# Reordering the first ten microseconds of an attention + MLP block: modulation products ahead of the transposes, weights loaded in smaller pieces over two queues, and dummy matmuls gated by statistics

## Chip, cores and metric

The kernel runs on one core of one Trainium2 chip. The metric is device time of one execution in microseconds (us). Each profile gives the *span* too, from the first to the last recorded instruction; here the time is some 1.75 us longer than the span. Three executions of the kernel before took 560.24, 560.35 and 560.86 us.

## The reference

One transformer block with adaptive layer norm: 2048 tokens of width 512, 32 query heads on 8 key/value heads of width 128, and an MLP of 1792. Everything is bf16.

```python
mod = (silu(c) @ w_mod).reshape(1, 6, 1, -1)          # c: (1, 512), w_mod: (512, 3072)
sa, ca, ga, sb, cb, gb = (mod[:, i] for i in range(6))
h = layernorm(x) * (1 + ca) + sa                      # modulated norm
x = x + ga * attention(h, k_cache, v_cache, wq, wo)   # q = h @ wq, softmax(q k^T) v @ wo
h = layernorm(x) * (1 + cb) + sb
return x + gb * (relu(h @ w1) @ w2)
```

`attention` here reads the last 512 of the 2048 cached positions. The attention loop cannot start before the first query tile is there. That needs x (normalized), c (through silu and two of the six modulation products), and the first query weights.

## The kernel before

All that the change touches lies in the prologue. In the traces the engines run their instructions in the order in which the program adds them (the tensor engine of before: seven dummies from 1.04 us, c at 4.95, nine dummies from 5.06, transposes from 8.82, products from 9.04); a helper attaches the semaphore waits.

```python
def load_wm01(i, eng=None):                # two halves of the first two modulation matrices
    c0, c1 = i * DC // 2, (i + 1) * DC // 2
    dma(wm01[:, c0:c1, :], wm01v[:, c0:c1, :], f"wm{i}", writes=[R_wm[i]], eng=eng)

def warm(n):                               # dummies: nothing reads their result
    for i in range(n):
        mm(bank[WBK], ones[:, :], ones[:, 0:1].to_broadcast([P, QB]), True, True, [R_ones], [WBK], i == n - 1)
# ... cut: layer norm helpers, the attention loop, the MLP
for i in range(2):                         # x of the first 512 tokens, one half on each queue
    dma(x_sb[:, 2 * i:2 * i + 2, :], xv[:, 2 * i:2 * i + 2, :], f"xa{i}", writes=R_x[2 * i:2 * i + 2], eng=ACT if i else SP)
dma(c_row[:, :], c[0].rearrange("(c p) -> c p", p=P), "c", writes=[R_c])
load_wm01(0)
load_wm01(1, ACT)
load_wq(0, 2, ACT)                         # query weights of heads 0 and 1
load_wq(2, 2)
load_k(0)
load_v(0)
kb.op(POOL, lambda e: e.memset(ones[:, :], 1.0), writes=[R_ones])
# ... cut: identity and constants on GpSimd
warm(7)
silu_exp(5)                                # transpose of c on the tensor engine, exp(-c) and a copy on ScalarE
warm(9)
# ... cut: the statistics of token tile 3 on ScalarE
silu_mul()                                 # three operations on GpSimd: silu of c
ln_stat(0)                                 # statistics of tiles 0..2 on VectorE
ln_stat(1)
rstd_add(0, 2)
rstd_pow(0, 2)                             # power -1/2 on GpSimd
ln_stat(2)
rstd_add(2, 3)
rstd_pow(2, 4)
ln_norm(0)
ln_norm(1)                                 # VectorE; tile 3 is normalized by GpSimd
ln_tposes(0, TB[0])                        # four 128x128 transposes of tile 0
fs = mod_cols_mm(0, QBK)                   # 32 modulation products, one column each
for f in fs:
    f()
ln_norm(2)
mod_cols_evac(0, QBK)
for tl in range(1, TPB):
    ln_tposes(tl, TB[tl // 2])
mod_half(0, 0, DVE)                        # scale and shift on the way out of PSUM
mod_half(0, 2, ACT)
mod_half(0, 1, DVE)
mod_half(0, 3, ACT)
q_half(0, 0, CC_ORDER, QBK)                # first query halves
# ... cut: the other halves, then the loop
```

The dummies are there so that the tensor engine's clock is at full instead of half rate when the real work begins; in before's trace 512-wide matmuls start 0.43 us apart from 1.45 to 8.45 us and 0.21 to 0.22 us apart from 13.56 us on. That dummies bring the full rate is an assumption of mine.

## Time and profile before

| | before |
|---|---|
| time, three executions | 560.24, 560.35, 560.86 us |
| the profiled execution | 561.1 us, span 559.4 us |
| tensor engine busy | 98% of the span |
| first exponential of the loop (ScalarE) | 13.76 us after the start |

The lines are in the prediction below. A row of the timeline reads: start, busy time, engine, source line, operation, output <- inputs, shapes, how many were merged, and in brackets how long the engine had been idle and what ended it.

### The profile page before, as it was taken

To read this page: it belongs to the slowest core of one execution; us is meant where nothing else is said; L and a number is where in the kernel's file an instruction comes from. 1 tells how busy PE (TensorE), PEld (TensorE's weight loads), DVE (VectorE), ACT (ScalarE), POOL (GpSimd) and SP (SyncE) were. 2 spreads that over 40 slices of the span, in tenths; PEclk is the share of its full clock that TensorE was granted. 3 is DMA by queue.
4 is the path that set the end of the run, shared out by engine and by line. 5 is a ranking of instruction groups with operands and counts; after the bars stand their busy time and mean duration, and the time that the engine had idled before them with its cause. 6 is when DMAs were issued, how large, how long until landed. Compare 5 with 4: busy or idle time off the path is not lost.

```text
span 559.4 us, 9666 instructions
## 1 busy us (share of the span) xinstructions
PE 550.5 (98%) x4060; PEld 315.8 (56%) x4134; DVE 253.8 (45%) x551; ACT 348.9 (62%) x453; POOL 54.7 (10%) x53
## 2 busy tenths in 40 slices
PE   8999999999999999999999999999999999999998
PEld 4665555555555555555555555555555654444444
DVE  4455555553546544335445443333354448321134
ACT  4986666666666666666666666666666644432500
POOL 3000022004410000033000000332000000000000
DMA  9897763513114144352352412111215110210001
GB/s 268 248 207 174 143 169 46 114 39 76 40 38 76 39 73 117 58 133 57 94 95 57 76 40 39 39 39 38 39 39 76 39 30 0 44 34 23 22 29 47
DMA packets 113309, 42.67 MB, mean 76 GB/s; under 512 B 93928, under 2 KB 112104, under 8 KB 113256
## 3 DMA queue, kind: packets, MB, share of 16 engines
q1 hardware_dynamic: 112024, 40.82, 34.3%
q10 hardware_dynamic: 1232, 1.15, 0.6%
q8 instruction: 33, 0.54, 0.4%
q14 instruction: 20, 0.16, 0.1%
HBM read 18.35 MB, written 2.10 MB: 37 GB/s over the span
## 4 chain that ended last, share of the span: by engine, by line
PE 98%; issue 1%; DMA 1%; DVE 0%; SPq 0%; DVEq 0%
PE psS L1372 28%; PE psO L1372 27%; PE psQ L1372 23%; PE psW L1372 20%; DMA c_row<-in_c_dram 1%; DVE qT L1611 0%; DVE hT L1630 0%; SPq L1303 0%; DVE PT L1723 0%; DVE PT L1725 0%; PE psS L1375 0%; PE psO L1416 0%; DVE modc L1438 0%; DVEq L123 0%
## 5 line engine op out<-in xcount | busy, mean ns | idle before, releaser
L1493 ACT ACTIVATE PT<-psS 128x1024 bf16<-128x1024 f32 x256 | 262.7, 1028 | 128.2 <-PE psS L1372 128.1
L1372 PE MATMUL psS<-qT,kT 128*128 128x512 bf16 x508 | 150.9, 379 | 0.5 <-DVE qT L1611 0.4
L1372 PEld LDWEIGHTS psO<-v,PT 128*128 128x128 bf16 x2048 | 126.6, 98 | 30.2
L1372 PE MATMUL psO<-v,PT 128*128 128x129 bf16 x2048 | 137.0, 220 | 0.0
L1372 PE MATMUL psQ<-hT,wq 128*128 128x512 bf16 (+1 forms) x510 | 130.5, 377 | 0.3 <-DVE hT L1630 0.2
L1503 DVE RECIPROCAL rinv<-psO 128x4 f32<-128x4 f32 x128 | 23.3, 182 | 227.2 <-PE psO L1372 227.2
L1372 PE MATMUL psW<-wo,oT 128*128 128x512 bf16 x454 | 118.1, 379 | 3.0
L1504 DVE TENSOR_TENSOR o<-psO,rinv 128x512 bf16<-128x512 f32 x128 | 88.5, 691 | 4.9 <-DVE rinv L1503 0.5
L1372 PEld LDWEIGHTS psQ<-hT,wq 128*128 128x128 bf16 x512 | 49.9, 98 | 60.3 <-issue 0.6
L1372 PEld LDWEIGHTS psS<-qT,kT 128*128 128x128 bf16 x512 | 49.5, 98 | 58.9 <-ACT PT L1493 0.7
L1485 ACT ACTIVATE qT<-psQ 128x512 bf16<-128x512 f32 x126 | 74.7, 593 | 0.0
L1712 ACT ACTIVATE wq<-psS 128x512 bf16<-128x512 f32 x56 | 33.4, 597 | 49.3 <-PE psS L1372 48.9
L1372 PEld LDWEIGHTS psW<-wo,oT 128*128 128x128 bf16 x512 | 45.0, 98 | 32.9 <-DVE acc L1526 1.2
L1526 DVE TENSOR_TENSOR acc<-psW,acc 128x512 f32<-128x512 f32 x48 | 33.2, 691 | 6.5 <-PE psW L1372 6.5
L1372 PE MATMUL psO<-wmw,wq 128*128 128x512 bf16 (+1 forms) x165 | 32.8, 352 | 0.3
L1529 POOL TENSOR_TENSOR acc<-acc,gaf 128x512 f32<-128x512 f32 x12 | 15.6, 1303 | 146.7 <-DVE acc L1526 139.8
L1388 POOL TENSOR_TENSOR rstd<-rstd,cst 128x4 f32<-128x4 f32 x7 | 7.2, 1025 | 216.8 <-DVE rstd L1387 216.8
L1723 DVE TENSOR_TENSOR PT<-psO,gbf 128x512 f32<-128x512 f32 (+1 forms) x12 | 7.5, 624 | 40.4 <-PE psO L1372 40.4
L1372 PE MATMUL psS<-h2T,wmw 128*128 128x512 bf16 x109 | 25.0, 379 | 0.2
L1372 PEld LDWEIGHTS psO<-wmw,wq 128*128 128x128 bf16 x168 | 15.3, 98 | 16.5
L1372 PE MATMUL psS<-hT,wmw 128*128 128x512 bf16 x110 | 24.4, 379 | 0.1
L1382 DVE BATCH_NORM_STATS2 st<-x 128x6 f32<-128x512 bf16 x31 | 21.1, 681 | 4.8 <-DMA x<-in_A_x_dram 4.8
(85 smaller groups left out, 192.6 us busy)
## 6 DMA issues: line engine op xcount, KB each, us to landing
wo<-in_A_wo_dram SPq DMA_DIRECT2D x4, 1024.0 KB, 5.9
wq<-in_A_wq_dram SPq DMA_DIRECT2D x7, 512.0 KB, 4.6
wmw<-in_B_w_dram SPq DMA_DIRECT2D x14, 256.0 KB, 3.1
wmw<-in_w_mod_dram SPq DMA_DIRECT2D x5, 512.0 KB, 4.8
oT<-o SPq DMA_TRANSPOSE x128, 2.4
out_dram<-PT SPq DMA_DIRECT2D x15, 128.0 KB, 1.7
x<-in_A_x_dram SPq DMA_DIRECT2D x3, 512.0 KB, 4.3
v<-in_A_v_cache_dram SPq DMA_DIRECT2D x8, 128.0 KB, 3.8
```

What stands on the lines that cost most here:

```text
L1372: kb.op(PE, lambda e: e.matmul(out_ap, lhsT, rhs, start=start, stop=stop), reads=reads, group_writes=[R_b[k] for k in bk], signal=signal)
L1382: kb.op(DVE, lambda e: e.bn_stats(st[:, t, :], x_sb[:, t, :]), reads=[R_x[t]], writes=[R_st[t]])
L1388: kb.op(POOL, lambda e: e.tensor_tensor(rstd[:, sl], rstd[:, sl], cst[:, 0:1].to_broadcast([P, hi - lo]), op=ALU.pow), reads=R_rstd[sl] + ...
L1485: kb.op(ACT, lambda e: e.activation(qT[u % NQT][:, :], bank[bk], ACTF.Copy), reads=[R_b[bk]], writes=[R_qT[u % NQT]])
L1493: kb.op(ACT, lambda e: e.activation(PT[u % NPT][:, pr * 2:pr * 2 + 2, :], s_ps[pr][:, :, :], ACTF.Exp, scale=scale), reads=[R_b[pr * 2], R ...
L1503: kb.op(DVE, lambda e: e.reciprocal(rinv[:, u, :], o_ps[:, :, P]), reads=[R_b[5], R_b[6]], writes=[R_rinv])
L1504: kb.op(DVE, lambda e: e.tensor_tensor(o_sb[u % NOS][:, :, :], o_ps[:, :, 0:P], rinv[:, u, :].unsqueeze(2).to_broadcast([P, TPB, P]), op=A ...
L1526: kb.op(DVE, lambda e: e.tensor_tensor(acc[:, tl, :], bank[WBK], acc[:, tl, :], op=ALU.add), reads=[R_b[WBK], R_acc[tl]], writes=[R_acc[tl]])
L1529: kb.op(eng, lambda e: e.tensor_tensor(acc[:, tl, :], acc[:, tl, :], gaf[:, :], op=ALU.mult), reads=[R_acc[tl], R_ga], writes=[R_acc[tl]])
L1712: kb.op(ACT, lambda e: e.activation(h1T[b % 2][:, fc, :], bank[bk], ACTF.Relu), reads=[R_b[bk]], writes=[R_h1[b % 2][fc]], pre=all_events( ...
L1723: kb.op(DVE, lambda e: e.tensor_tensor(yt[i][:, c0:c1], bank[bk][:, c0:c1], gbf[:, c0:c1], op=ALU.mult), reads=[R_b[bk], R_gb], writes=[R_ ...
```

## The change

Its intent is to shorten the start: put the products where the tensor engine waits for normalization anyway, get the weights for them earlier, and have the tensor engine at full clock (512-wide matmuls 0.21 us apart, not 0.43) by means of dummies that do not stand in the way. The loads, in four and two pieces on alternating queues, and the ones set by VectorE:

```diff
-    load_wm01(0)
-    load_wm01(1, ACT)
-    load_wq(0, 2, ACT)
+    for i in range(DC):
+        load_wm01(i, (ACT, SP)[i % 2])
+    for i, eng in enumerate((ACT, SP)):
+        dma(wq_sb[:, 2 * i:2 * i + 2, 0:QA * Dh], wqv[:, 2 * i:2 * i + 2, 0:QA * Dh], f"wqa{i}", writes=[R_wqa[i]], eng=eng)
     load_wq(2, 2)
...
-    kb.op(POOL, lambda e: e.memset(ones[:, :], 1.0), writes=[R_ones])
+    kb.op(DVE, lambda e: e.memset(ones[:, :], 1.0), writes=[R_ones])
```

The dummies, and the order (cut: the helpers take a gate, and waits name the pieces instead of the halves):

```diff
-    warm(7)
+    warm(10)
     silu_exp(5)
-    warm(9)
...
     ln_stat(0)
+    warm(3, [R_mv[0]])
     ln_stat(1)
+    warm(2, [R_mv[1]])
...
-    ln_tposes(0, TB[0])
     fs = mod_cols_mm(0, QBK)
     for f in fs:
         f()
+    ln_tposes(0, TB[0])
+    mod_cols_evac(0, QBK)
     ln_norm(2)
-    mod_cols_evac(0, QBK)
...
-    for tl in range(1, TPB):
-        ln_tposes(tl, TB[tl // 2])
+    ln_tposes(1, TB[0])
+    warm(2, bk=6)
+    ln_tposes(2, TB[1])
+    ln_tposes(3, TB[1])
+    warm(1, bk=6)
```

Below, "the loads", "the order", "the gated dummies" (10, then 3 and 2) and "the dummies between" (2 and 1 among the transposes) name these parts.

More of the change, by code (lines that the diff above doesn't have):

```diff
@@ L1319, in build_fast @@
     R_q1 = RL("q1_", 2)
+    R_wmc = RL("wmc", DC)
+    R_wqa = RL("wqa", 2)
     R_cf, R_m01 = Res("cf"), Res("m01")
@@ L1350, in load_wm01 @@
     def load_wm01(i, eng=None):
-        c0, c1 = i * DC // 2, (i + 1) * DC // 2
-        dma(wm01[:, c0:c1, :], wm01v[:, c0:c1, :], f"wm{i}", writes=[R_wm[i]], eng=eng)
+        dma(wm01[:, i, :], wm01v[:, i, :], f"wmc{i}", writes=[R_wmc[i]], eng=eng)
     def wm_res(sl, cc):
-        return R_wm[cc // (DC // 2)] if sl < 2 else R_wm[sl]
+        return R_wmc[cc] if sl < 2 else R_wm[sl]
     def load_wo(j):
@@ L1363, in load_mlp @@
         if not wm_done:
-            wm_done.extend(all_events(R_wm))
+            wm_done.extend(all_events(R_wm + R_wmc))
         f0 = i % (FC // 2) * 2
@@ L1375, in tpose, with warm @@
         kb.op(PE, lambda e: e.transpose(out_ap, in_ap, ident[:, :]), reads=list(reads) + [R_ident], group_writes=[R_b[k] for k in bk], signal=signal)
-    def warm(n):
+    def warm(n, gate=(), bk=7):
         for i in range(n):
-            mm(bank[WBK], ones[:, :], ones[:, 0:1].to_broadcast([P, QB]), True, True, [R_ones], [WBK], i == n - 1)
+            mm(bank[bk], ones[:, :], ones[:, 0:1].to_broadcast([P, QB]), True, True, [R_ones] + list(gate), [bk], i == n - 1)
     def ln_stat(t):
@@ L1480, in q_mms @@
             mm(bank[bk], wq_sb[:, cc, h * Dh:(h + 1) * Dh], hT[b % 2][:, cc, :], i == 0, i == DC - 1,
-               [R_wq[h], R_hT[b % 2][cc]] + ([R_h0[cc]] if b == 0 else []), [bk], i == DC - 1)
+               (R_wqa if h < QA else [R_wq[h]]) + [R_hT[b % 2][cc]] + ([R_h0[cc]] if b == 0 else []), [bk], i == DC - 1)
         q_evac(u, bk)
@@ L1636, in q_half @@
             mm(bank[bk][:, hf * HB:(hf + 1) * HB], wq_sb[:, cc, u * Dh:(u + 1) * Dh], hT[0][:, cc, hf * HB:(hf + 1) * HB], cc == CC_ORDER[0], cc == CC_ORDER[-1],
-               [R_wq[u], R_half[hf][cc]], [bk], cc == CC_ORDER[-1])
-    for tl in range(1, TPB):
-        ln_tposes(tl, TB[tl // 2])
+               [R_wqa[cc // 2], R_half[hf][cc]], [bk], cc == CC_ORDER[-1])
+    ln_tposes(1, TB[0])
[3 more added lines that the diff above has]
+    warm(1, bk=6)
     mod_half(0, 0, DVE)
@@ L1712, in h1_group @@
         kb.op(ACT, lambda e: e.activation(h1T[b % 2][:, fc, :], bank[bk], ACTF.Relu), reads=[R_b[bk]], writes=[R_h1[b % 2][fc]],
-              pre=all_events(R_wq) if b < 2 else ())
+              pre=all_events(R_wq + R_wqa) if b < 2 else ())
     def y_group(b, tl, c0=0, c1=D, deng=None):
```

## The prediction

> **What bounds the kernel now.** I read the page first, then the chain of waits in order of time for the first 20 us, then the timeline of the first 30 us, then busy time and DMA by stretches of one microsecond. The page:
>
> ```profile
> span 559.4 us, 9666 instructions
> PE 550.5 (98%) x4060; PEld 315.8 (56%) x4134; DVE 253.8 (45%) x551; ACT 348.9 (62%) x453; POOL 54.7 (10%) x53
> PE 98%; issue 1%; DMA 1%; DVE 0%; SPq 0%; DVEq 0%
> ```
>
> The tensor engine is busy all the time and is 98% of the chain, so no other engine's speed matters except where it holds up the tensor engine. The diff touches nothing after the first two query projections: the attention loop, the output projection and the MLP keep their instructions and their order, as a listing of both kernels' instruction order confirms. What can change is therefore the start. The chain for it (start us, us, what):
>
> ```profile
> 1.24 3.66 DMA c_row<-in_c_dram
> 4.95 0.18 PE psO L1416
> 5.13 3.86 PE psW L1372 x9
> 8.98 0.22 PE psS L1375 x4
> 9.21 0.79 PE psQ L1372 x32
> 10.02 0.18 DVE modc L1438
> 10.30 0.42 DVE hT L1630
> 10.86 0.78 PE psQ L1372 x4
> 11.64 0.89 PE psO L1372 x8
> 12.55 0.44 DVE qT L1611
> 13.34 0.38 PE psS L1372
> ```
>
> psW x9 are dummy matmuls on a tile of ones, psS x4 the transposes of token tile 0, psQ x32 the modulation products, psQ/psO after them the first query halves; psS at 13.34 is the first score matmul, where the real loop begins. From there 559.4 - 13.34 = 546 us follow that the change leaves alone. So all that can be won lies in 13.34 us, 2.4% of the span, and a good part of that waits for x and c to land near 4.9 us. The timeline shows what the dummies hide (start us, us, engine line op tiles):
>
> ```profile
> 5.43 0.28 POOL L1421 TENSOR_SCALAR tmp<-tmp 128x4 f32<-128x4 f32 x1 [3.17 <-ACT c_f L1418]
> 5.80 1.04 POOL L1422 TENSOR_TENSOR tmp<-tmp,cst 128x4 f32<-128x4 f32 x1
> 6.92 0.20 POOL L1423 TENSOR_TENSOR sc_bf<-c_f,tmp 128x4 bf16<-128x4 f32 x1
> 7.08 1.51 POOL L1591 TENSOR_TENSOR rstd<-rstd,cst 128x2 f32<-128x2 f32 x2
> 7.82 1.22 DVE L1393 TENSOR_SCALAR xn<-x,mv,rstd 128x512 bf16<-128x512 bf16 x3
> 8.70 0.90 POOL L1604 TENSOR_SCALAR xn<-x,s,rstd 128x512 bf16<-128x512 bf16 x1
> 10.28 1.47 ACT L1632 ACTIVATE hT<-psS,modc 128x256 bf16<-128x256 bf16 x3 [2.87 <-PE psS L1375]
> ```
>
> Behind the dummies a second chain runs through GpSimd: silu of c (three operations, done at 7.12), two rstd powers, then the normalization of tile 3. VectorE has tile 0 normalized at about 7.82 + 0.41 = 8.23, but the tensor engine is inside its nine dummies until about 8.8. ScalarE then idles 2.87 us: it has no modulation before the products and their evacuation, and the products sit behind the transposes of tile 0.
>
> [...] in the early dummies the weight loads start 0.42 to 0.43 us apart, in the loop four 512-wide psQ matmuls take 1.02 us with one tail of 0.38, so (1.02 - 0.38)/3 = 0.21 us apart. (The granted-clock column says 1.00 in both, so I judge by spacing.) The doubling comes near the ninth dummy of the second group, at some 8.7 us. [...] 385, 378 and 366 GB/s in the three microseconds from 4 to 7[...].
>
> **The change, part by part.**
> *Loads.* The first two modulation matrices come in four quarters, alternating over both queues, instead of two halves, and the first two heads' query weights come in two halves, one per queue. Before, the later half of the modulation weights was issued at 1.66 us and took the longest of that tile's times to landing, 6.3 us: 7.9 us. After, x (0.52 MB) and the four quarters (1.05 MB) are first in line; the stretches move 0.03 MB to 2 us, 0.58 MB from 2 to 4 us, then 0.385, 0.378 and 0.366 MB per us, so 1.57 MB are there at about 6.6 us. Estimated landing 6.7 us instead of 7.9. By itself it saves nothing, as the products ran at 9.04; it allows the new order.
> *Ones set by VectorE instead of GpSimd.* First dummy at about 1.0 instead of 1.04 us: nothing.
> *Ten dummies instead of seven before the transpose of c.* 1.0 + 0.40 + 9 x 0.427 = 5.24 us, where c lands at 4.90. The transpose of c thus moves from 4.95 to about 5.24: 0.3 us later, and the whole GpSimd chain with it, as no slack is in it (silu done 7.42, first rstd pair 8.08, second 8.9, tile 3 normalized 9.0 to 9.9; VectorE's tile 0 at 8.12 to 8.53, tile 1 to 8.86). This is the cost that I think the change carries.
> *Nine dummies become 3 gated by tile 0's statistics and 2 gated by tile 1's.* With the statistics at 5.70 and 6.49 and full clock, they end near 6.4 and 6.95; at half clock 3 x 0.427 and 2 x 0.427 run to 7.03 and 7.88. Either way they no longer reach 8.8.
> *Products before the transposes.* They start at 7.47 (silu + 0.05), last 0.8 us (32 at 25 ns) and end near 8.3, while VectorE still normalizes. Removed from the path between transposes of tile 0 and the others: the 0.8 us. Evacuation goes between tile 1 and tile 2 on VectorE, at about 8.8 to 8.95.
> *Transposes and three more dummies.* Tile 0 at 8.6, tile 1 at 8.93 to 9.15; two dummies (0.43 us at full clock) to 9.6; tile 2 (normalized 8.97 to 9.38) to 9.82; tile 3 must wait for GpSimd's 9.9, so 10.0 to 10.22; one dummy to 10.43. The first two dummies fall into time in which tile 3 is awaited anyway; the last costs 0.2 us, except that the modulation of the first half finishes about then: VectorE 9.40 to 10.13 (0.33 us apart), ScalarE 9.40 to 10.42 (0.46 apart).
> *Query halves.* 10.43 instead of 10.86: eight matmuls at 0.11 to 11.3; the second half's modulations start at 10.46, when tile 3 is in PSUM, and VectorE's third ends at about 11.5 (before: 11.99); unit 0's second half ends at 11.68, before at 12.35. **Sum: 0.67 us earlier**, so the first score matmul at about 12.65 to 12.7.
> From there ScalarE (2 x 1.03 + 0.59 = 2.65 us a unit) and the tensor engine (8 x 0.215 + 16 x 0.057 = 2.63 us a unit) run as before and everything is shifted. 560.35 - 0.7 = 559.6 us.
>
> **The rivals.**
> *A, no delay of c:* if the clock opens inside the ten dummies[...], or c lands late as well, the 0.3 us fall away, tile 3 is ready at 9.6, and the score starts near 12.35: 559.3 us.[...]
> *B, the clock opens late or falls back:* the new second group is only 5 dummies with gaps[...]. If the array is at half clock at 10.4 us, sixteen 256-wide matmuls cost 16 x 0.107 = 1.7 us more and the first loop matmuls some more: 561 to 562.[...]
> *C, a load takes the place of the wait:* the K load is issued some 0.8 us later behind the extra issues on SyncE. Its bytes are still behind the same bytes, it took 7.2 us at most from 2.62, so 9.8, and even 10.6 is before 12.65. Query weights landed by 9.3 (2.1 + 7.1) before and are needed at 10.4. I expect no wait, 0.0 us.
> *D, gated on tile 3:* GpSimd's normalization is the bound whatever the order, and only the end of it counts: then gain is 10.46 - 10.2 = 0.2 us, and the time is 560.1. Against it: 0.8 us of products no longer stand in line with it, and the modulation of the first half no longer waits for the third tile.
>
> **How range and chances follow.** Sum 0.7, A 1.0, D 0.2, B a loss of 1 to 1.5. The three times before lie within 0.6 us of each other, so I take 558.7 to 560.7 as the range for 8 in 10, with 559.6 as the time. A gain of 2% would be 11.2 us, most of the prologue, 4.9 us of which are the landing of inputs: 1%. A loss of 2% needs the clock to stay at half for over 20 us: 1%. Within 2%: 98%.
>
> **What would show it.** Right: the transpose of c near 5.24 us; products from about 7.5 us and ahead of all transposes; no dummy running at 8.5 us; tile 3 the last awaited transpose, near 10.0; query halves from 10.4; first score matmul at 12.5 to 12.8; spacing 0.21 us in the loop from there and a span near 558.7. Wrong: dummies or query matmuls 0.43 (or 0.21 for 256 columns) apart after 9 us (B); products waiting for a quarter of the modulation weights after 7.5, or query matmuls for a DMA (C); c transposed at 4.95 (A); or a loop that takes more or less than 546 us, which my account excludes.

Its sum came to 0.67 us earlier, rounded to 0.7, and so to 560.35 - 0.7 = 559.6 us. Cut, as marked, are reasons that no run of this case shows: for what opens the clock and lets it fall back, and for how two queues share the transfers.

## The result

The changed kernel took 561.44 us in the median of six executions (560.75 to 562.79), the kernel before 560.54 us in its six (560.24 to 561.53). The ratio was 1.0016, with a 95% interval of 1.0002 to 1.0031. A ratio is the mean time of one kernel's runs over that of the other's of the same rounds, so it is not quite the ratio of these medians. The class predicted as all but certain, within 2%, came true; the direction did not. I had predicted 559.6 us and a range up to 560.7, and the result lies 1.8 us above the one and 0.7 above the other.

The page of the changed kernel has the same tensor engine, 98% busy:

```profile
span 559.6 us, 9674 instructions
PE 550.6 (98%) x4061; PEld 315.8 (56%) x4136; DVE 254.2 (45%) x552; ACT 349.1 (62%) x453; POOL 54.5 (10%) x52
PE 97%; DMA 1%; issue 1%; SPq 0%; DVE 0%
```

The chain of waits of the changed kernel at its start (start us, us, what):

```profile
2.06 6.91 DMA wmw<-in_w_mod_dram
...
9.01 0.35 PE psQ L1373 x8
9.36 0.47 PE psS L1376 x8
...
12.97 0.59 PE psS L1373 x2
```

Where the chain before went through nine dummies, it now goes through a load: the last quarter of the modulation weights, issued at 2.06 us, landed at 8.96 us, and the last eight products waited for it. The timeline of the changed kernel adds what came before:

```profile
1.11 4.45 PE L1373 MATMUL psW<-ones 128*128 128x512 bf16 x10 [1.11 <-DVE ones L1570]
5.49 0.18 PE L1417 MATMUL psO<-ident,c_row 4*128 4x4 bf16 x1
5.76 1.73 PE L1373 MATMUL psW<-ones 128*128 128x512 bf16 x5
...
7.72 0.92 PE L1373 MATMUL psQ<-sc_bf,wmw 128*128 128x1 bf16 x24 [0.23 <-POOL sc_bf L1424]
...
13.60 1.02 ACT L1494 ACTIVATE PT<-psS 128x1024 bf16<-128x1024 f32 x1 [1.25 <-PE psS L1373]
```

The transpose of c is at 5.49 us (before: 4.95), the products begin at 7.72 ahead of all transposes, and the first exponential is at 13.60 instead of 13.76. I compare by the exponential and not by the first score matmul: before, the records show one score matmul (psS) ahead of the next group, 0.42 us before the exponential; after, two of them, 0.63 us before it. The missing 0.21 us is one 512-wide matmul, so I infer that the record of the first one is missing in the trace of before, and that the 13.34 of my prediction should have been 13.13.

So in these two profiles the start became 0.16 us shorter, yet the span some 0.27 us longer (559.63 against 559.36). The difference lies near 510 us, where each engine takes a branch. In the list of that line's instructions (line, engine, instruction, min/median/max ns, start), before and after:

```profile
L1830 PEldq COMPARE_BRANCH  x1: 3440/3440/3440, 510.6 to 510.6; - x1
```

```profile
L1836 PEldq COMPARE_BRANCH  x1: 3880/3880/3880, 510.5 to 510.5; - x1
```

Behind the branch of 3.44 us the timeline shows no idle time of the tensor engine; behind that of 3.88 us it shows 0.46 us:

```profile
514.43 2.98 PE L1373 MATMUL psQ<-wmw,wq 128*128 128x512 bf16 x13 [0.46 <-issue]
```

Is that branch a property of the change? And is one profile of each kernel a fair pair at all? These were the first questions for the experiments.

### The profile page after: what moved, and what is told of

Read it like the earlier page. It is cut to its first block, busy times and chain, and to the rows that moved or that the text cites. A ratio compares the mean times of both kernels' runs of the same rounds, so it can differ in the third digit from the quotient of the medians.

```text
span 559.6 us, 9674 instructions
## 1 busy us (share of the span) xinstructions
PE 550.6 (98%) x4061; PEld 315.8 (56%) x4136; DVE 254.2 (45%) x552; ACT 349.1 (62%) x453; POOL 54.5 (10%) x52
## 4 chain that ended last, share of the span: by engine, by line
PE 97%; DMA 1%; issue 1%; SPq 0%; DVE 0%
PE psS L1373 28%; PE psO L1373 27%; PE psQ L1373 23%; PE psW L1373 19%; DMA wmw<-in_w_mod_dram 1%; SPq L1303 0%; PE psS L1376 0%; DVE qT L1614 0%; DVE PT L1729 0%; DVE PT L1731 0%; PE psW L1376 0%
```

## The experiments

**Theories.** (1) *The wait that I removed is not in the usual run*: the clock opens at a different time in each run, and the profiled run of before was one with a late opening. (2) *Load theory*: the quarters land too late and take the place of the dummies. (3) *Dummy theory*: ten dummies delay c, and those between the transposes lie on the path. (4) *Clock theory*, rival B of the prediction: with fewer dummies the clock falls back. (5) *Branch theory*: the longer branch (3.88 us against 3.44) belongs to the larger program. (6) Something outside the span, as the time minus the span had grown. "Theory 3" in the later expectations stands for (1) and (4) together: that the dummies decide when the clock opens and whether it falls back. Reasons given there for the clock and for the branch that no run shows are cut, as marked. Eighteen runs of kernels followed, on five chips; every one was correct. In the table, "out" is the mean of time minus span, and "low" counts runs whose mean granted clock was 0.993 to 0.997 instead of 0.999 or more. The granted clock reads 1.00 up to its first record (before and after read 1.00 in every stretch from 0 us on, though their early dummies start 0.43 us apart, and seven_first, with full clock from 11.85 us on, has a mean of 1.00), so "low" counts half-clock stretches after the opening and says nothing of a late opening. Kernels are compared with before on the same chip only. The rounds of one chip share the runs of before.

| chip | kernel | runs | mean us | mean span | out | low | ratio to before (95%) |
|---|---|---|---|---|---|---|---|
| 10 | before | 11 | 561.10 | 559.37 | 1.73 | 1 | |
| 10 | after_again | 6 | 561.44 | 559.43 | 2.00 | 1 | 1.0009 (0.9995 to 1.0022) |
| 10 | loads_only | 6 | 561.25 | 559.28 | 1.97 | 1 | 0.9999 (0.9983 to 1.0015) |
| 10 | order_only | 6 | 560.91 | 559.17 | 1.74 | 0 | 0.9994 (0.9981 to 1.0008) |
| 10 | dummies_only | 6 | 561.77 | 560.03 | 1.74 | 2 | 1.0012 (0.9994 to 1.0030) |
| 14 | before | 9 | 560.43 | 558.68 | 1.76 | 0 | |
| 14 | seven_first | 5 | 562.96 | 560.96 | 2.00 | 2 | 1.0049 (1.0035 to 1.0063) |
| 14 | old_loads | 5 | 561.37 | 559.64 | 1.73 | 1 | 1.0017 (1.0003 to 1.0031) |
| 14 | two_more | 5 | 560.71 | 558.98 | 1.73 | 0 | 1.0005 (0.9991 to 1.0019) |
| 14 | x_four_semaphores | 5 | 560.51 | 558.76 | 1.75 | 0 | 1.0000 (0.9986 to 1.0013) |
| 15 | before | 11 | 560.82 | 559.07 | 1.74 | 1 | |
| 15 | eight_seven_order | 6 | 560.39 | 558.63 | 1.75 | 0 | 0.9992 (0.9979 to 1.0005) |
| 15 | eight_seven_between | 6 | 561.12 | 559.37 | 1.75 | 2 | 1.0007 (0.9990 to 1.0024) |
| 15 | fourth_on_scalar | 6 | 560.65 | 558.92 | 1.73 | 0 | 0.9997 (0.9983 to 1.0012) |
| 15 | loads_three_on_scalar | 6 | 560.59 | 558.78 | 1.81 | 0 | 0.9996 (0.9983 to 1.0008) |
| 3 | before | 11 | 560.96 | 559.22 | 1.74 | 1 | |
| 3 | after_third | 5 | 561.30 | 559.30 | 2.00 | 1 | 1.0008 (0.9993 to 1.0022) |
| 3 | after_fourth | 5 | 561.17 | 559.20 | 1.97 | 0 | 1.0005 (0.9992 to 1.0018) |
| 3 | between_only | 5 | 560.95 | 559.20 | 1.75 | 0 | 1.0000 (0.9985 to 1.0014) |
| 3 | gated_only | 6 | 561.80 | 560.05 | 1.75 | 3 | 1.0014 (0.9999 to 1.0029) |
| 4 | before | 11 | 561.04 | 559.31 | 1.73 | 1 | |
| 4 | quarters_only | 6 | 561.03 | 559.13 | 1.89 | 0 | 0.9996 (0.9984 to 1.0008) |
| 4 | eight_seven_again | 6 | 561.13 | 559.40 | 1.73 | 2 | 0.9997 (0.9984 to 1.0009) |

Most intervals include 1: the effects are a tenth of a per cent, and verdicts rest on the traces more than on these ratios. "Out" is the exception; it varies far less than the time. In the profiles the landmarks were (us; "clock opens" is the trace's record of the full clock being granted, in brackets where it comes from the spacing of the dummies: before and order_only have no record, but before's dummies start 0.43 us apart up to 8.45 us and its transposes from 8.82 us on 0.05 to 0.06, against 0.10 to 0.11 for those at half clock in loads_only; "products" runs from the start of the first to that of the last):

| profile | clock opens | c transposed | modulation weights complete | products | first query half | first exponential | branch, ns | span |
|---|---|---|---|---|---|---|---|---|
| before | (8.8) | 4.95 | 7.91 | 9.04 to 9.82 | 10.86 | 13.76 | 3440 | 559.4 |
| after | 6.76 | 5.49 | 8.96 | 7.72 to 9.20 | 10.89 | 13.60 | 3880 | 559.6 |
| after_again | 3.81 | 4.84 | 7.92 | 7.06 to 8.16 | 9.98 | 12.70 | 3703 | 558.5 |
| after_third | 6.81 | 5.49 | 7.94 | 7.72 to 8.51 | 10.65 | 13.36 | 3343 | 558.9 |
| after_fourth | 3.77 | 4.67 | 8.41 | 6.95 to 8.65 | 10.28 | 12.99 | 3783 | 558.9 |
| x_four_semaphores | 6.57 | 4.56 | 8.51 | 8.56 to 9.35 | 10.39 | 13.28 | 3743 | 559.2 |
| fourth_on_scalar | 3.86 | 4.61 | 7.81 | 8.19 to 8.96 | 10.00 | 12.89 | 3640 | 558.7 |
| loads_only | 10.01 | 5.04 | 7.80 | 9.39 to 10.25 | 11.29 | 14.19 | 3600 | 559.9 |
| order_only | none recorded | 5.05 | 8.08 | 8.98 to 9.81 | 11.04 | 13.95 | 3460 | 559.6 |
| dummies_only | 7.07 | 5.49 | 8.22 | 9.07 to 9.85 | 11.19 | 13.90 | 3783 | 559.8 |
| between_only | 4.30 | 4.64 | 8.22 | 8.57 to 9.35 | 10.69 | 13.40 | 3620 | 559.2 |
| seven_first | 11.85 | 4.64 | 8.43 | 7.72 to 8.69 | 11.65 | 14.47 | 3563 | 560.2 |

In every profile the span is the time of the first exponential, plus one constant for the loop, plus what the branch takes beyond 3.44 us (or less what it falls short of it): over all twenty profiles the constant was 545.58 to 545.65 us. The account that the loop keeps its length is thus right, and everything is either in the prologue, in the branch, or outside the span.

### after_again, after_third, after_fourth: the changed kernel, unchanged

Edit: none. They ask how much one profile is worth.

> The changed kernel once more, on one chip beside the kernel before. Theory 1 (its parts cost): mean 0.4 to 1.1 us above the kernel before; some of its runs, about a third, have a mean granted clock of 0.997[...] and are 1 to 1.6 us longer than its others; in the profile the fourth quarter of the modulation weights lands after 8.5 us and c is transposed near 5.5 us, and the tensor engine's branch takes 3.8 to 3.9 us against 3.44 before. Theory 2 (chance of the first chip): difference within 0.2 us, no run at a lower clock, landing near 6.7 to 7.9 us.

> The changed kernel a third time. Theory 3[...]: in some of its profiles and runs the array falls back to half clock[...] after having opened; if the profile catches one, the fallback lies in the prologue or the first loop steps, before 15 us[...]. About a quarter of runs at 0.997, 1 to 1.5 us longer. Rival: the fallback lies elsewhere in the span (for instance at the branch near 510 us), and has nothing to do with the dummies. Branch 3.7 to 3.9 us if it belongs to the program, 3.4 to 3.9 if it is chance. Time minus span 2.0 us.

> As the third, for more runs and one more profile of the same program.

The same program on three more occasions opened its clock at 3.81, 6.81 and 3.77 us and had its first exponential at 12.70, 13.36 and 12.99. The last quarter landed at 7.92, 7.94 and 8.41. The branch took 3.70, 3.34 and 3.78 us: it is not a property of the program. Against before on their chips the spans were 0.06, 0.08 and -0.02 us longer, so the whole change gains nothing inside the span, on the mean, where I had predicted 0.67 us. I had expected 0.4 to 1.1 us of loss in time and a third of the runs at a lower clock; the means lost 0.2 to 0.3 us, and 2 of these 16 runs were low.

The run with a late opening and an early load shows what bounds the start when no load does. The chain of waits of after_third:

```profile
1.10 4.45 PE psW L1373 x10
5.55 0.13 PE psO L1417
...
7.67 0.67 POOL rstd L1592
...
8.36 0.42 DVE xn L1394
...
8.83 0.72 PE psS L1376 x8
9.55 0.43 PE psO L1373 x2
...
10.60 0.22 PE psO L1373
```

It runs from the ten dummies through c, the silu and the power on GpSimd and the normalization of tile 0, and then along the tensor engine with the three dummies among the transposes, 0.43 + 0.22 us. That they stand in the chain does not mean that the time would be saved without them: the timeline has GpSimd on tile 3 from 9.24 for 0.90 us, so it was ready at 10.14, and its transposes began at 10.21 whether or not two dummies ran before. between_only, below, gives the measured cost. What counts here is the first half: c at 5.49.

### loads_only, order_only, dummies_only: one part each

```diff
 # loads_only: before, with
-    load_wm01(0)
-    load_wm01(1, ACT)
-    load_wq(0, 2, ACT)
+    for i in range(DC):
+        load_wm01(i, (ACT, SP)[i % 2])
+    for i, eng in enumerate((ACT, SP)):
+        dma(wq_sb[:, 2 * i:2 * i + 2, 0:QA * Dh], ..., f"wqa{i}", writes=[R_wqa[i]], eng=eng)
 # order_only: before, with
-    ln_tposes(0, TB[0])
     fs = mod_cols_mm(0, QBK)
     for f in fs:
         f()
-    ln_norm(2)
+    ln_tposes(0, TB[0])
     mod_cols_evac(0, QBK)
+    ln_norm(2)
 # dummies_only: before, with warm(10), gated warm(3) and warm(2) in place of warm(7) and warm(9),
 # warm(2) and warm(1) among the transposes, and ones set by VectorE
```

> The kernel before with only the new loads (modulation weights in quarters on both queues, first query weights in halves). Theory 1: more and smaller loads let the 16 engines drift apart; the last modulation quarter lands at 8.5 to 9.0 us instead of 7.9, just in front of the products at 9.04, so the time is 0 to 0.3 us above the kernel before; tensor branch 3.4 us[...]; no run at 0.997. Rival (the late landing in the profile of the changed kernel was chance): last quarter before 8 us, time equal within 0.1 us.

> The kernel before with only the products ahead of the transposes of tile 0 and the evacuation ahead of tile 2's normalization. The nine dummies still run to 8.8 us, so products 8.9 to 9.7 us, transposes after them; first half's modulation starts near 10.0 instead of 10.3. Theory 1: gain 0.0 to 0.2 us, branch 3.4 us, no run at 0.997. Rival (order is worth as much as I had predicted): gain 0.5 us or more.

> The kernel before with only the dummies of the change (ten first, 3 and 2 gated by statistics, 2 and 1 between and after the transposes, ones set by VectorE). Theory 1: this part carries the loss: c transposed at 5.49 instead of 4.95 us, branch about 3.9 us, a third of runs at 0.997; mean 0.4 to 1.2 us above the kernel before. Rival (the loss sits in the loads): equal within 0.2 us and all runs at 1.0.

None is told from before by its time. Two things stand out. Time minus span is 1.97 us in loads_only, as in the full change, and 1.74 us in the two others, as in before: what was lost outside the span, 0.25 us, comes with the loads. And dummies_only has two of six runs at 0.997, with spans of 561.3 and 561.2. In its profile the products stay behind the transposes of tile 0, and these wait for VectorE until 8.83 us, no earlier than before (8.82): with c at 5.49 the normalization is later, and the removed dummies bring nothing. In loads_only the last quarter landed at 7.80 us, where I had expected 8.5 to 9.0, so quarters are not late by themselves. In order_only the nine dummies took 4.02 us, at half clock by their spacing, and held the products back to 8.98.

### seven_first: the changed kernel with c not delayed

```diff
 # on the changed kernel
-    warm(10)
+    warm(7)
```

> The changed kernel with seven dummies instead of ten before the transpose of c. Theory 1 (ten dummies hold c back and with it silu, statistics powers and tile 3): where the clock opens after the dummies, c is transposed near 5.0 instead of 5.49 us and the first score matmul comes 0.3 to 0.5 us earlier than in the changed kernel's profile (12.97); mean span 0.2 to 0.5 us below the changed kernel's 559.5. Counter-effect: [...]the clock opens later (8 to 10 us) in more runs. Rival (the load of the modulation weights is the wait that counts): span unchanged within 0.1 us. Time minus span 2.0 us as in the changed kernel.

The obvious repair, seven dummies ahead of c as before, was the worst kernel: 562.96 us, a ratio of 1.0049. c was transposed at 4.64 us, but the clock stayed at half until 11.85. The timeline of its tensor engine:

```profile
5.61 2.31 PE L1373 MATMUL psW<-ones 128*128 128x512 bf16 x5 [0.79 <-DVE mv L1384]
...
8.71 1.01 PE L1376 MATMUL psS<-ident,xn 128*128 128x128 bf16 x8
```

The five gated dummies begin only when tile 0's statistics are there, after 0.79 us of idling, and they take 2.31 us, 0.43 us apart; the eight transposes take 1.01 us where the same eight take 0.72 in after_third. So in this profile, with seven dummies, a pause and five dummies, the clock was not open before 11.85 us; in the four profiles of the changed kernel, with ten in front, it opened at 3.77 to 6.81. By these five profiles the three extra dummies in front are what is lacking here, and they are the ones that delay c: in this kernel one part of the change needs the other.

### old_loads: order and dummies without the loads

```diff
 # on the changed kernel
-    for i in range(DC):
-        load_wm01(i, (ACT, SP)[i % 2])
-    for i, eng in enumerate((ACT, SP)):
-        dma(wq_sb[:, 2 * i:2 * i + 2, 0:QA * Dh], ..., f"wqa{i}", writes=[R_wqa[i]], eng=eng)
+    load_wm01(0)
+    load_wm01(1, ACT)
+    load_wq(0, 2, ACT)
```

> The changed kernel with the loads of the kernel before. Theory 1: time minus span goes back from 2.0 to 1.73 us, as the extra loads cost 0.27 us outside the span; products wait for the later half, which lands at 7.9 to 8.2 us, instead of the fourth quarter at 7.9 to 9.0; span the same within 0.3 us; total 0.2 to 0.5 us below the changed kernel. Rival (quarters were needed for the order): span 0.3 us or more longer.

Time minus span is back at 1.73 us. The span is 0.96 us longer than before on this chip, where all nine runs of before were short (558.4 to 558.9). In its profile the clock opened at 6.51, c was transposed at 5.49, the weights were complete at 8.19, the products ran at 8.33 and the first exponential came at 13.60. This is the same first exponential as in the first profile of the changed kernel, with the load in halves: either way a load of these weights, needed at 7.5, is not there.

### two_more: two dummies more, in the kernel before

```diff
 # on before
-    warm(7)
+    warm(9)
```

> The kernel before with nine instead of seven dummies in its first group, that is two more instructions on the tensor engine and nothing else; c is still transposed at about 5.0 us. Theory 1[...]: the tensor branch near 510 us takes 3.7 to 3.9 us instead of 3.44, and the mean span is 0.2 to 0.4 us above the kernel before. Rival (the branch's time is chance of a run): 3.44 to 3.5 us, span equal within 0.2 us.[...]

c was transposed at 5.00 us instead of 4.56 to 4.95, and the time was 0.28 us above before, within the interval. The branch took 3.54 us. Two instructions more did not bring the 3.7 to 3.9 us that the branch theory expected. With 3.34 to 3.88 us in four profiles of one unchanged program, that theory falls.

### x_four_semaphores: more loads, more semaphores, the same prologue

```diff
 # on before; only the later three blocks of x, far from the start
     def load_x(b):
-        dma(x_sb[:, b * TPB:(b + 1) * TPB, :], ..., f"x{b}", ...)
+        for i in range(TPB):
+            t = b * TPB + i
+            dma(x_sb[:, t:t + 1, :], xv[:, t:t + 1, :], f"x{b}_{i}", writes=[R_x[t]])
```

> The kernel before with each of the three later loads of x, which come well ahead of their use in the attention loop, cut into four loads with a semaphore each: nine more loads and nine more semaphores, nothing on the critical path. Theory 1 (the 0.27 us outside the span in the changed kernel come with its three additional loads with semaphores of their own): time minus span 1.73 + 9 x 0.09 = 2.5 us, span unchanged within 0.2 us. Rival (they come from loads on ScalarE's queue or from chance): time minus span stays at 1.73 us.

Nine more loads, each with a semaphore of its own, left time minus span at 1.75 us. The number of loads or semaphores does not explain the 0.25 us.

It gave something better by accident. Its first 20 us are those of before, instruction for instruction, and in its profiled run the clock opened at 6.57 us. Its tensor engine in the timeline:

```profile
4.68 3.04 PE L1374 MATMUL psW<-ones 128*128 128x512 bf16 x9
...
8.56 0.95 PE L1374 MATMUL psQ<-sc_bf,wmw 128*128 128x1 bf16 x32
...
10.39 0.78 PE L1374 MATMUL psQ<-hT,wq 128*128 128x256 bf16 x4 [0.18 <-DVE hT L1632]
```

and its chain of waits in the same stretch:

```profile
1.65 6.86 DMA wmw<-in_w_mod_dram
...
8.56 0.97 PE psQ L1374 x32
```

The nine dummies took 3.04 us instead of the 3.92 us of before's profile and were over by 7.7. They held nothing back; the products waited for their weights, landing at 8.51. The first exponential was at 13.28, 0.48 us earlier than in before's profile and 0.32 earlier than in after's. This is the usual run of before: of 53 executions of it, 35 had spans of 558.4 to 559.1 us and 18 of 559.3 to 560.7 (the branch is in these too, so they sort by the clock only roughly); the one that I had read, at 559.4, was of the second kind. With the constant above, and even with the shortest branch seen (3.34 us), a span of 559.1 us leaves 559.1 - 545.6 + 0.1 = 13.6 us for the first exponential, less than the 13.76 that I had read.

### fourth_on_scalar and loads_three_on_scalar: which queue

```diff
 # fourth_on_scalar: before, with
-    load_wq(2, 2)
+    load_wq(2, 2, ACT)
 # loads_three_on_scalar: loads_only, with both halves of the query weights on SyncE
-    for i, eng in enumerate((ACT, SP)):
+    for i, eng in enumerate((SP, SP)):
```

> The kernel before with the load of the query weights of heads 2 and 3 issued by ScalarE instead of SyncE: four loads on ScalarE's queue as in the changed kernel, the same number in all. Theory (the fourth load on ScalarE's queue makes the 0.27 us outside the span): time minus span 2.0 us, span equal within 0.3. Rival (another thing about the loads makes it): 1.73 us.

> The kernel before with the change's loads, but both halves of the first query weights on SyncE's queue, so that ScalarE issues three loads as before. Theory (fourth load on ScalarE): time minus span 1.73 us. Rival (the quarters or their semaphores): 2.0 us. Fourth quarter lands 7.8 to 9.0 us either way.

A fourth load on ScalarE's queue, which the change has and before has not, costs nothing outside the span by itself (1.73 us). With only three there, the changed loads still have 1.81. So the loads' cost outside the span shrinks but does not go, and the theory of the fourth load, which expected 2.0 and 1.73, falls.

fourth_on_scalar also shows before's order with an early clock: opened at 3.86, first exponential at 12.89. The changed kernel at the same opening had 12.70 and 12.99.

### eight_seven_order, eight_seven_between, eight_seven_again: can a part be kept?

```diff
 # eight_seven_order and eight_seven_again: order_only, with
-    warm(7)
+    warm(8)
     silu_exp(5)
-    warm(9)
+    warm(7)
 # eight_seven_between: the same, with warm(2) and warm(1) among the transposes as in the change
```

> A version made from the findings: the loads of the kernel before, products ahead of the transposes, eight dummies before the transpose of c and seven right after it, none gated and none between transposes. Theory 3[...]: clock opens before 7.2 us or so in every run, c near 4.6 to 5.0, products from 7.9 to 8.5 when the second half of the modulation weights lands, first exponential of unit 1 at 15.0 to 15.6 against 15.6 to 16.05 in the kernel before; mean span 0.3 to 0.9 us below the kernel before, time minus span 1.73. Rival (the prologue's order and clock do not move the end): equal within 0.2 us.

> The same with the change's dummies between and after the transposes (two and one). Theory 3: they cost at most 0.2 us in the path and save some runs from falling back to half clock[...]: fewer runs at 0.997, mean span equal to the version without within 0.3 us. Rival (they only cost): 0.2 to 0.4 us longer, fallbacks as often.

> The version made from the findings (old loads, products first, eight and seven dummies) once more. Theory 3: no run or one below clock 1.0, mean span 0.1 to 0.6 us below the kernel before on the same chip, first score matmul at 12.2 to 12.9 us[...]. Rival (its lead of 0.4 us on the last chip was chance): equal within 0.1 us or behind.

The first looked like a gain: 560.39 us against 560.82, but with an interval that includes 1. In its profile the clock opened at 4.33 us, c was transposed at 4.61 and the weights were complete at 7.79, nearly as in fourth_on_scalar with the old order (3.86, 4.61, 7.81); the first exponential came at 12.85 against 12.89. With c undelayed and an early clock the new order is worth 0.04 us in this pair of profiles: the products wait for the weights until 7.93, and the transposes behind them for VectorE's tile 2. The repeat on another chip gave 561.13 against 561.04, with two runs at a lower clock. Together they show nothing ahead of before, and no version is. In the repeat's profile the clock opened at 4.11 and fell back from 10.93 to 14.35 us; its first exponential was at 14.53. eight_seven_between, where I had expected the dummies to save runs from a lower clock, had 2 of 6 such runs; in its profile (opened at 5.78) the first exponential came at 12.84. The three runs of this group had 4 executions in 18 at a lower clock, without a gated dummy among them.

### between_only and gated_only: which dummies

```diff
 # between_only: before, with
-    for tl in range(1, TPB):
-        ln_tposes(tl, TB[tl // 2])
+    ln_tposes(1, TB[0])
+    warm(2, bk=6)
+    ln_tposes(2, TB[1])
+    ln_tposes(3, TB[1])
+    warm(1, bk=6)
 # gated_only: before, with warm(10) for warm(7), no warm(9), and
     ln_stat(0)
+    warm(3, [R_mv[0]])
     ln_stat(1)
+    warm(2, [R_mv[1]])
```

> The kernel before with only the two dummies between the transposes and the one after them. Theory 3: fallback no more often than in the kernel before (4 of its 31 runs on three chips below 1.0), span 0.1 to 0.4 us longer, because the query halves start behind one more dummy. Rival (it is these dummies that go with the fallback, as 10 of 34 runs of versions with them fell back, among them 2 of 6 without any gating): a quarter or more of the runs at 0.997, mean 0.4 us or more longer.

> The kernel before with only the first two groups of dummies changed: ten before the transpose of c, three and two gated by statistics, none between the transposes. Theory 3[...]: a quarter or more of the runs at 0.997, mean span 0.3 us or more above the kernel before; c at 5.49 us. Rival (the dummies between transposes go with the fallback): no run below 1.0, mean span within 0.3 us.

The dummies between the transposes alone cost nothing that five runs can show. Its profile says how much: products from 8.57 us and the exponential at 13.40, where two profiles with the same prologue but for them have 8.56 and 13.28 (x_four_semaphores), 8.58 and 13.29 (two_more), so some 0.11 us between single profiles. The gated ones seem to cost, though the interval of the ratio just includes 1: three of six runs had spans of 560.3 to 561.3 at a clock of 0.994 or 0.997, the three others 559.2 to 559.7 at 1.0. The profile fell into one of the first kind. By stretches (us, then busy time and instructions of PE, PEld, DVE, ACT, POOL, then granted clock, DMA share, GB/s):

```profile
6.10:9.40 3.30, 1.64 (x25) 0.83 (x24) 2.42 (x9) 1.70 (x6) 3.03 (x6) 1.00 1.24 287
9.50:12.80 3.30, 3.30 (x39) 2.77 (x37) 1.96 (x7) 1.86 (x4) 0.58 (x1) 0.50 1.16 301
12.90:16.30 3.40, 3.23 (x20) 1.45 (x19) 0.93 (x3) 2.02 (x4) 0.00 (x0) 1.00 1.16 326
```

and the timeline of its tensor engine:

```profile
8.77 0.40 PE L1375 MATMUL psS<-ident,xn 128*128 128x128 bf16 x4 [1.66 <-DVE xn L1393]
...
11.92 1.50 PE L1372 MATMUL psO<-hT,wq 128*128 128x256 bf16 x8
```

In the 3.30 us before, the tensor engine was busy for 1.64; the granted clock was then 0.50 from 9.45 to 12.86 us, that is for 3.41 us, and the eight query matmuls took 1.50 us instead of 1.04. Such a stretch at half clock is 3.41 x 0.5 / 560 = 0.003 of the span, which is the 0.997 of this run in the list. By this estimate every 0.997 in that list is a run with one such stretch, and they can be counted without a trace; where in the span it lay, and how long it was, is shown only by the two profiles that caught one, from 9.45 us here and from 10.93 to 14.35 (3.42 us) in eight_seven_again. Kernels with the gated dummies (the changed kernel's 22 runs, dummies_only, gated_only, old_loads, seven_first) had 12 in 44; before and the versions that keep its two groups ahead of and behind c, with their nine ungated dummies (loads_only, order_only, two_more, x_four_semaphores, fourth_on_scalar, loads_three_on_scalar, between_only, quarters_only), 5 in 98. The eight_seven kernels, in neither group, had their 4 in 18, so such stretches come without gated dummies too. In gated_only such runs were some 1.2 us longer than the rest (560.67 against 559.43).

### quarters_only: the smaller pieces of one tensor

```diff
 # before, with the modulation weights in quarters and the query weights as before
-    load_wm01(0)
-    load_wm01(1, ACT)
+    for i in range(DC):
+        load_wm01(i, (ACT, SP)[i % 2])
     load_wq(0, 2, ACT)
```

> The kernel before with the modulation weights in quarters on both queues and the first query weights in one load on ScalarE's queue as before, so four loads on ScalarE. Theory: the time outside the span (2.0 us with the change's loads, 1.81 with both query halves on SyncE, 1.73 with the old loads, also with a fourth load on ScalarE or nine more loads and semaphores) comes with the quarters: 1.9 to 2.0 us. Rival: it comes with the halves of the query weights over both queues: 1.73 us. Span within 0.3 us of the kernel before.

Time minus span was 1.89 us. The two partial versions of the loads thus have 0.16 us (this one, quarters of the modulation weights alone) and 0.07 us (loads_three_on_scalar) more than before on their chips, the whole has 0.25. These do not add up to a rule, and no record here shows what happens outside the span; the cause stays open.

## Why the prediction was wrong

Its mechanism was right in outline: only the prologue moves, the loop keeps its length, the products fit into the wait for normalization, the transposes follow. The sum failed by three of its terms, one rival was given too little, and two terms were missing from it.

1. **"What can change is therefore the start", read from one profile.** This step failed most. The nine dummies that ran to 8.8 us are a feature of a late clock, which opened at 8.8 there and at 6.57 and 3.86 in two profiles with before's order. In these two the products waited for their weights (8.51) or the transposes for VectorE (7.95), and there is no 0.8 us of dummies to remove. At equal opening the change brings nothing to the first exponential: 13.60 and 13.36 against 13.28 at about 6.7 us, 12.70 and 12.99 against 12.89 at about 3.8. Over the records of all profiles the opening lies anywhere from 3.77 to 11.85 us, and for the changed kernel alone from 3.77 to 6.81; I had fitted to one. The 0.75 us between the profiled run and the median was the warning. The change is not without effect, though: in all seven profiles of kernels with ten dummies in front the clock was open by 7.07 us, while with seven and nine it opened at 8.8 us or later in four of eight; and the changed kernel's runs with a mean clock of 1.0 have spans of 559.6 us at most, before's of up to 560.2. By these counts, which are small, it takes away the late openings and loses about as much in the other runs.
2. **"First dummy at about 1.0" and "The transpose of c thus moves from 4.95 to about 5.24".** It moved to 5.49 where the clock opened near 6.8 (to 4.84 and 4.67 where it opened near 3.8). VectorE's ones were done at 1.05, the first dummy began at 1.11, the second 0.40 us later and the tenth at 4.92; with one more distance of 0.427 I estimate that it was through at 5.35, and another 0.14 us went by before the transpose. Against a run of before in which c landed early (4.56) the delay is 0.93 us, not 0.29, and in after_third it stands on the chain in full: c, silu, power, normalization, transposes. loads_three_on_scalar is the nearest pair to it, with before's order and dummies and quarters that were complete at 7.84 us against 7.94: with c at 4.59 and an opening at 6.40 its first exponential came at 12.97, not 13.36.
3. **"Estimated landing 6.7 us instead of 7.9", and rival C's "I expect no wait, 0.0 us".** The last quarter landed at 8.96, 7.92, 7.94 and 8.41 us. I had added up bytes as if the transfers came in order. In the first profile they do not: the 16 landings recorded for that quarter run from 6.71 to 8.96 us, while the first part of the query weights, issued 0.14 us after it on the other queue, was there at 7.11. (Before, the 16 of the later half run from 6.58 to 7.91.) Cutting the halves in two did not bring the end forward at all: the weights were complete at 7.80 to 8.96 us in the eight profiles with quarters and at 7.65 to 8.51 in the twelve with halves. In the first profile the total rate in the three microseconds from 4 to 7 was also lower than before (334, 332, 302 GB/s against 385, 378, 366). Rival C worked out K and the query weights only, though the list of what would show me wrong has this wait, "products waiting for a quarter of the modulation weights after 7.5"; the load that took the wait's place was the one whose earlier arrival the change was meant to bring.
4. **The dummies among the transposes, "the first two dummies fall into time in which tile 3 is awaited anyway; the last costs 0.2 us".** This step held. In after_third tile 3 was ready at 10.14 us and its transposes began at 10.21, dummies or not, and between_only lost some 0.11 us.
5. **Rival B, "the clock opens late or falls back".** My argument against it was not shown by any run and is cut. The fall came after 3.30 us with 1.64 us busy in gated_only (longest idle time 1.66 us), which is far from idle, and after a fuller stretch in eight_seven_again (2.49 of 3.30, with an idle time of 1.82 us that ended in it, at 8.28). What sets it is not found: fourth_on_scalar's stretch from 7.27 to 10.68 us holds the same instructions as the latter (16 transposes, 32 products, the first five query matmuls; busy for 2.64 of 3.41 us against 2.52 from 7.52 to 10.93), and its clock stayed full (1.0 in the run list). It came in 4 of 22 runs of the changed kernel, against 4 of 53 of before; over all kernels with gated dummies, 12 of 44. At 1.2 us each the difference is worth an estimated (4/22 - 4/53) x 1.2 = 0.13 us on the mean. These are small counts; only the 12 in 44 against 5 in 98 is a clear difference.
6. **Outside the sum altogether:** 0.27 us between span and time (2.0 against 1.73 to 1.76), which comes with the loads. Inside the span the repeats of the change and before are within 0.1 us of each other, so this term is most of what their means lost (0.34, 0.34 and 0.21 us). On the first chip the means lie 0.92 us apart; 0.27 of it is this term, and two of the changed kernel's six runs were low.
7. **The branch** near 510 us was not the change's: on the tensor engine it took 3.34 to 3.88 us in four profiles of one program (50 to 72 ns on the four other engines, listed in three of these), and 3.44 in before's lies inside that. In the first pair it added 0.44 us to the wrong side.

What stays open: why the loads cost time outside the span, what opens the clock, and what makes it fall back.

## What to carry to other kernels

Before removing a wait, look at several runs of it: if the run that was profiled is slower than the median, the wait may belong to that run and not to the kernel. Each part of a prologue that is tuned around dummies (when c is transposed, how many dummies, what gates them) can lose more elsewhere than it gains; seven_first shows it at its worst: c 0.85 us earlier than in the first profile of the changed kernel, the clock open 5.09 us later, and 1.0049 of before's time. When a transfer is moved earlier, ask for the landing of its slowest piece (here 8.96 us, where the first was there at 6.71), not for the bytes in line ahead of it.
